# One chunk's state output product by Strassen's identity, with its block sums made beside the matmuls

## The chip, the cores and the metric

The kernel runs on one core of a Trainium2 chip. The metric is device time in microseconds (us). TensorE (PE) multiplies, VectorE (DVE) and ScalarE (ACT) do elementwise work, GpSimd (POOL) and SyncE (SP) issue most of the DMAs. The engines run beside one another and meet only at semaphores. TensorE writes into PSUM, which has eight banks of 128 partitions by 512 float32.

## The reference

A sequence of 2048 tokens of 512 features is normalized. Beside a residual connection it goes through a state space layer (A) and a gated feed-forward layer (B), and the three are added.

```python
def reference(A_x, ...):
    def _A_ref(x, ...):
        Lam_bar = jnp.exp(dt * Lam)
        B_bar = ((Lam_bar - 1.0) / Lam)[:, None] * Bmat
        Bu = jnp.einsum("bld,pd->blp", x + 0j, B_bar)
        for t in range(L):
            h = Lam_bar[None, :] * h + Bu[:, t, :]
            hs.append(h)
        hseq = jnp.stack(hs, 1)
        return 2.0 * jnp.einsum("blp,dp->bld", hseq, Cmat).real + x * Dskip[None, None, :]

    def _B_ref(x, w_gate, w_up, w_down):
        return (_silu(x @ w_gate) * (x @ w_up)) @ w_down

    xn = _layernorm(A_x, axis=-1)
    return A_x + _A_ref(xn, ...) + _B_ref(xn, ...)
```

The state is complex with 512 entries, so the last product of A is a real one: 2048 tokens by 1024 (real and imaginary parts) times 1024 by 512.

## The kernel before

The 2048 tokens are four chunks of 512, and each chunk is four tiles of 128 tokens, numbered `n` = 0 to 15. For each chunk the kernel makes the input projection of the state (`bproj`), the recurrence on VectorE (a rotation, eight scans, a rotation back into `w_tiles[c]`, called `wt` in the profile), the gate and up projections (`gateup`), the down projection into one PSUM bank per tile, and at last adds the state's output product into the same bank (`out_ssm`): eight matmuls of 512 columns per tile, one for each 128 of the 1024 state rows, `wt` against `CF`. The last 96 of the 1376 features of the feed-forward layer are treated apart: they are moved by small DMAs into `gu_rows` and enter through 32-row matmuls (`out_rows`).

The order is written out by hand. VectorE's recurrence steps stand in a backlog; `pump` issues some of them between matmuls, and `need("ssm2")` issues all that are left of chunk 2. What an engine or a queue is given it does in that order.

The first half (chunks 0 and 1) comes up in `out_chunk(1)`, before chunk 3's gate and up projections. The outputs of tiles 0 to 7 are copied out of PSUM by ScalarE into a buffer `res` of the pool `opool`, which has six of them, and added into the output in HBM by an accumulating DMA on GpSimd's queue (`out_leave`); the output in HBM already holds the residual, and `skip_store` adds the skip term there. Chunks 2 and 3 come up at the end, in `out_pair(2)`: the eight tiles 8 to 15 take all eight PSUM banks, first ten down-projection matmuls for each (80 in all), then `out_rows`, then `out_ssm` for chunk 2 and for chunk 3. Chunk 2's tiles leave by `out_leave`; chunk 3's by a VectorE addition with `xn_end` (which by then holds skip and residual) and plain stores from ScalarE's and SyncE's queues. The last tile, 15, is treated apart, so that little is left behind the last matmul: VectorE adds its bank to `xn_end` into `part_end` before the state product, and the state product goes into three fresh banks of 256, 128 and 128 columns, the blocks of `out_blocks`.

`CT` holds the transposed raw `C`, from which `CF` is made on VectorE during chunk 0. `BT` holds the transposed `B` for `bproj`; after the last `bproj` its real part is overwritten with the last rows of the down weights (`wd_rows`). `wg_g[2]` and `wu_g[2]` hold the gate and up weights of four of the eleven feature tiles; chunk 3's projection is their last reader. `jidx` is a float32 tile of 128x512, read only when the tables of sines are made, early. `pm` is a pool of three VectorE buffers of 4 KB per partition.

Of the kernel before, what the change touches and what calls it, by code (L numbers as in the profile page):

```python
# [10 lines left out]
F32 = mybir.dt.float32  # L11
BF16 = mybir.dt.bfloat16
ALU = mybir.AluOpType
ACT = mybir.ActivationFunctionType
# [9 lines left out]
def kernel(  # L24
# [17 lines left out]
    nc = tc.nc  # L42
    _, L, D = A_x.shape
# [4 lines left out]
    HW = CW // 2  # L48
    NT = L // 128
    NCH = L // CW  # L50
    TPC = CW // 128
    KD = D // 128
    HK = KD // 2
    NQ = Pst // 128
# [11 lines left out]
    ssm = ctx.enter_context(tc.tile_pool(name="ssm", bufs=1))  # L66
    gut = ctx.enter_context(tc.tile_pool(name="gut", bufs=2))
    up_p = ctx.enter_context(tc.tile_pool(name="up_p", bufs=4))
    opool = ctx.enter_context(tc.tile_pool(name="opool", bufs=6))
# [4 lines left out]
    def bank(shape=(128, CW), dtype=F32):  # L74
        return psum.tile(list(shape), dtype, name="ps")

    def flat(ap3):
        return ap3.rearrange("p q j -> p (q j)")

    x_v = A_x[0].rearrange("(n p) d -> p n d", p=128)  # L80
    out_v = out[0].rearrange("(n p) d -> p n d", p=128)
# [8 lines left out]
    wg_g, wu_g = [], []  # L90
# [7 lines left out]
    BT = const.tile([128, 2, KD, Pst], BF16, name="BT")  # L98
    CT = const.tile([128, 2, NQ, D], BF16, name="CT")
# [3 lines left out]
    CF = const.tile([128, 2, NQ, D], BF16, name="CF")  # L103
# [12 lines left out]
    HD = D // 2  # L116
# [51 lines left out]
    jidx = const.tile([128, CW], F32, name="jidx")  # L168
# [7 lines left out]
    part_end = const.tile([128, D], F32, name="part_end")  # L176
# [22 lines left out]
    xn_end = const.tile([128, TPC, D], BF16, name="xn_end")  # L199
# [72 lines left out]
    V = nc.vector  # L272
# [99 lines left out]
    u_tiles, w_tiles = {}, {}  # L372
# [85 lines left out]
    def gu_tile(c):  # L458
        if c not in gu_tiles:
            gu_tiles[c] = gut.tile([128, FT - 1, CW], BF16, name="guT")  # L460
        return gu_tiles[c]

    def u_tile(c, fi):
        if (c, fi // 2) not in u_pair:
            u_pair[c, fi // 2] = up_p.tile([128, 2, CW], BF16, name="u2")
        return u_pair[c, fi // 2]

    def product(c, fi):
        g, u = gu_tile(c)[:, fi - 1:fi + 1, :], u_tile(c, fi)[:]
        products.append(lambda: V.tensor_tensor(out=g, in0=g, in1=u, op=ALU.mult))  # L470
# [23 lines left out]
    def up_halves():  # L494

        pss = []
        for c in range(0, NCH, 2):
            ps = bank()
            pss.append(ps)
            for k in range(KD):  # L500
                for i in range(2):
                    nc.tensor.matmul(ps[i * LB:(i + 1) * LB], lhsT=wu_last[:, k, :],  # L502
                                     rhs=xnT[:, k, (c + i) * CW:(c + i + 1) * CW], start=(k == 0), stop=(k == KD - 1))
        for c in range(NCH):
            i = c % 2
            nc.scalar.copy(out=ul(c)[0:LB, :], in_=pss[c // 2][i * LB:(i + 1) * LB])
        product_last(0)
        product_last(1)
# [36 lines left out]
    o_tiles = {}  # L545

    def out_blocks(n):

        return ((0, D // 2), (D // 2, D - 128), (D - 128, D)) if n == NT - 1 else ((0, D),)

    def out_rows(c, step):

        for i in range(TPC):
            n, rows = c * TPC + i, slice(i * RT, (i + 1) * RT)
            nc.tensor.matmul(o_tiles[n][0][:], lhsT=gu_rows[c][rows, step, :], rhs=wd_rows[rows, step, :],  # L555
                             start=False, stop=(step == 2 and (c == 0 or n == NT - 1)))

    def out_pair(c):

        multiply(0)  # L560
        for n in range(c * TPC, (c + 2) * TPC):
            o = bank()
            o_tiles[n] = [o]
            k, i = divmod(n, TPC)
            for fi in range(FT - 1):
                nc.tensor.matmul(o[:], lhsT=gu_tiles[k][:, fi, i * 128:(i + 1) * 128], rhs=wd_sb[:, fi, :],  # L566
                                 start=(fi == 0), stop=False)
            pump(FT * 0.2163)
        for step in range(3):
            for k in (c, c + 1):  # L570
                out_rows(k, step)
        need(f"ssm{c}")
        need("skip")
        for n in range(c * TPC, (c + 1) * TPC):
            out_ssm(n)
            pump(2 * NQ * 0.2163)
        need(f"ssm{c + 1}")
        n = NT - 1
        o = o_tiles[n][0]
        V.tensor_tensor(out=part_end[:], in0=o[:], in1=xn_end[:, TPC - 1, :], op=ALU.add)  # L580
        o_tiles[n] = [bank((128, hi - lo)) for lo, hi in out_blocks(n)]
        for n in range((c + 1) * TPC, (c + 2) * TPC):
            out_ssm(n)

    def out_ffn(n):
        c, i = divmod(n, TPC)
        o_tiles[n] = []
        for lo, hi in out_blocks(n):
            o = bank((128, hi - lo))
            o_tiles[n].append(o)  # L590
            for fi in range(FT - 1):
                nc.tensor.matmul(o[:], lhsT=gu_tiles[c][:, fi, i * 128:(i + 1) * 128], rhs=wd_sb[:, fi, lo:hi],  # L592
                                 start=(fi == 0), stop=False)

    def out_ssm(n):
        c, i = divmod(n, TPC)
        if c > 0:
            res = opool.tile([128, D], BF16, name="res")
        for o, (lo, hi) in zip(o_tiles[n], out_blocks(n)):
            fresh = n == NT - 1  # L600
            o = o[:, 0:hi - lo]
            for part in range(2):
                for q in range(NQ):
                    nc.tensor.matmul(o, lhsT=w_tiles[c][:, part, q, i * 128:(i + 1) * 128],  # L604
                                     rhs=CF[:, part, q, lo:hi], start=(fresh and part == 0 and q == 0),
                                     stop=(c > 0 and part == 1 and q == NQ - 1))
            if c == NCH - 1:
                rest = part_end[:, lo:hi] if fresh else xn_end[:, i, lo:hi]
                V.tensor_tensor(out=res[:, lo:hi], in0=o, in1=rest, op=ALU.add)  # L609
                for a, b in ((0, D // 2), (D // 2, D)) if i == 0 else ((lo, hi),):  # L610
                    late = b == D and n in (NT - TPC, NT - 1)
                    (nc.sync if late else nc.scalar).dma_start(out=out_v[:, n, a:b], in_=res[:, a:b])
            elif c > 0:
                out_leave(n, o, res)

    def out_leave(n, o, res):
        nc.scalar.copy(out=res[:], in_=o[:])  # L617
        nc.gpsimd.dma_start(out=out_v[:, n, :], in_=res[:], accum_op=ALU.add)  # L618
# [14 lines left out]
    def step():  # L633
        for item in backlog[0:AHEAD + 1]:
            if item[2] is not None:
                item[2]()
                item[2] = None
        cost, op, _, _ = backlog.pop(0)
        op()
        owed[0] -= cost  # L640

    def pump(us):

        owed[0] += us
        while backlog and owed[0] >= backlog[0][0] * 0.5:
            step()
        if not backlog:
            owed[0] = 0.0

    def multiply(keep):  # L650

        while len(products) > keep:
            products.pop(0)()
            owed[0] -= 0.65

    def need(tag):

        while any(item[3] == tag for item in backlog):
            step()
# [135 lines left out]
    for fis in (range(4, EARLY - 1), range(EARLY - 1, EARLY)):  # L795
        ps, n = bank(), len(fis)
# [21 lines left out]
    def out_chunk(c):  # L818

        multiply(0)  # L820
        for n in range(c * TPC, (c + 1) * TPC):
            out_ffn(n)
            pump(FT * 0.2163)
        if c == 0:
            need("ln3")
            up_halves()
            multiply(0)
        if c == 1:
            for step in range(3):
                for k in range(2):  # L830
                    out_rows(k, step)
            for n in range(TPC):
                out_leave(n, o_tiles[n][0], opool.tile([128, D], BF16, name="res"))
        need(f"ssm{c}")
        need("cf")
        for n in range(c * TPC, (c + 1) * TPC):
            out_ssm(n)
            pump(2 * NQ * 0.2163)
# [46 lines left out]
    nc.sync.dma_start(out=out[0, 0:(NT - TPC) * 128, :], in_=A_x[0, 0:(NT - TPC) * 128, :])  # L885
    queue_ssm(2)
    out_chunk(0)
    gateup_chunk(2)
    bproj_chunk(3)
    load_rows()  # L890
    for c in range(NCH):
        queue("skip", [(1.2, lambda c=c: skip_op(c)),
                       (0.0, lambda c=c: skip_store(c)) if c < NCH - 1 else (1.2, skip_add)])
    queue_ssm(3)
    out_chunk(1)
    gateup_chunk(3)
    out_pair(2)


# [28 lines left out]
```

## Time and profile before

| | us |
|---|---|
| median of the three timed runs | 178.75 |
| the three runs | 178.48 to 178.84 |
| span of the profiled execution, first to last instruction | 176.8 |

The timed figure covers some 2 us around the span. The profile is of one execution. It is read from the page (busy times, the chain of work that ended last, the costliest groups) and from answers of the trace: the timeline, in which successive instructions of one kind are merged into a row with their count, groups of instructions by shape, and DMAs with their time from the start of the issuing instruction to landing. A matmul's shown length holds the way through the array, so rows of matmuls are read by the distance of their starts.

### The profile page before, as it was taken

Reading aid. Unit: us, or ns where it says so; the run is one execution under the profiler, and the core shown is the slowest. Engines: PE = TensorE matmul, PEld = TensorE weight load, DVE = VectorE, ACT = ScalarE, POOL = GpSimd, SP = SyncE. Lnnn points to the kernel's source line nnn. Section 1 sums busy time; section 2 is a strip of 40 time slices with the busy share of each in tenths; the row PEclk is TensorE's granted clock in tenths of the full one; section 3 lists DMA queues with packets and bytes.
Section 4 is the critical chain, followed back from the end, with each engine's and each line's share of the span. In section 5 each row is a group of like instructions: output and inputs, shape, how many; then the busy total and the mean of one; then the engine's idle time right before and its main releaser. Section 6 shows DMA issues by size and latency. Waiting matters only on the chain.

```text
span 176.8 us, 2598 instructions
## 1 busy us (share of the span) xinstructions
PE 172.1 (97%) x939; PEld 83.4 (47%) x954; DVE 153.8 (87%) x235; ACT 96.4 (55%) x178; POOL 51.8 (29%) x86
## 2 busy tenths in 40 slices
PE   8999999999999999999999999999999999999993
PEld 3877544444444444444444444444444444444443
DVE  4779998999999997999999999999999999981033
ACT  5397899867698679714666661053866610001300
POOL 6050120001400220019998040058476510001410
PEclk9999999999999999999999999999999999999999
DMA  5998497995431013900000020029799300000652
GB/s 164 305 186 197 91 247 97 336 272 117 88 73 21 0 30 89 356 4 17 17 19 19 0 85 7 0 23 126 88 126 188 64 6 0 0 4 0 64 99 75
DMA packets 31292, 16.36 MB, mean 92 GB/s; under 512 B 20208, under 2 KB 31088, under 8 KB 31248
## 3 DMA queue, kind: packets, MB, share of 16 engines
q1 hardware_dynamic: 24704, 11.51, 27.5%
q0 software_dynamic: 5184, 4.07, 16.0%
q10 hardware_dynamic: 1392, 0.62, 1.2%
q8 instruction: 7, 0.11, 0.3%
q14 instruction: 5, 0.04, 0.1%
HBM read 8.33 MB, written 5.24 MB: 77 GB/s over the span
## 4 chain that ended last, share of the span: by engine, by line
PE 94%; DMA 2%; issue 1%; SPq 0%; DVE 0%
PE ps L455 35%; PE ps L604 16%; PE ps L380 16%; PE ps L566 10%; PE ps L592 10%; DMA wu<-in_B_w_up_dram 2%; PE ps L693 2%; PE ps L513 2%; PE ps L774 2%; PE ps L555 2%; PE ps L502 1%; PE ps L245 0%; SPq L113 0%; SPq L123 0%; DVE res L609 0%
## 5 line engine op out<-in xcount | busy, mean ns | idle before, releaser
L455 PE MATMUL ps<-xnT,wu 128*128 128x512 bf16 (+1 forms) x144 | 36.3, 373 | 0.2
L455 PE MATMUL ps<-xnT,wg 128*128 128x512 bf16 (+1 forms) x145 | 36.3, 373 | 0.2
L422 DVE TENSOR_TENSOR_SCAN g<-r_t,car,u 128x512 bf16<-128x512 f32 x24 | 28.8, 1263 | 0.0
L380 PE MATMUL ps<-xnT,BT 128*128 128x512 bf16 x126 | 28.2, 379 | 0.1
L604 PE MATMUL ps<-CF,wt 128*128 128x512 bf16 (+2 forms) x140 | 27.6, 355 | 0.4 <-issue 0.3
L474 ACT ACTIVATE guT<-ps 128x512 bf16<-128x512 f32 (+1 forms) x40 | 23.6, 590 | 5.9 <-PE ps L455 5.8
L475 ACT CAST u<-ps 128x512 bf16<-128x512 f32 (+1 forms) x40 | 23.0, 576 | 6.5 <-PE ps L455 6.4
L617 ACT CAST res<-ps 128x512 bf16<-128x512 f32 x12 | 6.7, 590 | 36.1 <-PE ps L604 26.8
L455 PEld LDWEIGHTS <-wu 128*128 128x128 bf16 x148 | 14.5, 98 | 16.6
L188 POOL DMA_DIRECT2D gu_rows<-ul x36 | 17.7, 499 | 15.8 <-DVE ul L490 15.8
L455 PEld LDWEIGHTS <-wg 128*128 128x128 bf16 x148 | 14.4, 98 | 16.5
L382 ACT CAST u<-ps 128x512 bf16<-128x512 f32 x32 | 18.2, 586 | 6.0 <-PE ps L380 5.9
L618 POOL DMA_DIRECT2D out_dram<-res x12 | 10.5, 1221 | 36.2 <-ACT res L617 36.1
L604 PEld LDWEIGHTS <-wt 128*128 128x128 bf16 x144 | 13.3, 98 | 15.0 <-issue 1.3
L380 PEld LDWEIGHTS <-BT 128*128 128x128 bf16 x128 | 12.5, 98 | 14.9 <-issue 0.3
L214 POOL TENSOR_TENSOR rstd<-ve,neg_half 128x2 f32<-128x2 f32 (+1 forms) x4 | 5.7, 1418 | 44.9 <-DVE ve L213 44.9
L592 PE MATMUL ps<-wd_sb,guT 128*128 128x512 bf16 x79 | 17.5, 379 | 0.1
L566 PE MATMUL ps<-wd_sb,guT 128*128 128x512 bf16 x79 | 17.4, 379 | 0.1
L470 DVE TENSOR_TENSOR guT<-guT,u 128x1024 bf16<-128x1024 bf16 x20 | 13.4, 678 | 0.0
L566 PEld LDWEIGHTS <-guT 128*128 128x128 bf16 x80 | 7.8, 98 | 9.5
L592 PEld LDWEIGHTS <-guT 128*128 128x128 bf16 x80 | 7.8, 98 | 9.5
L205 DVE BATCH_NORM_STATS2 stats<-xall 128x6 f32<-128x512 bf16 x14 | 9.5, 678 | 2.7 <-DMA xall<-in_A_x_dram 2.7
(125 smaller groups left out, 201.4 us busy)
## 6 DMA issues: line engine op xcount, KB each, us to landing
out_dram<-in_A_x_dram SPq DMA_DIRECT2D x1, 1536.0 KB, 6.9
out_dram<-res POOLq DMA_DIRECT2D x12, 128.0 KB, 3.5
out_dram<-xall POOLq DMA_DIRECT2D x3, 512.0 KB, 8.4
wd_sb<-in_B_w_down_dram SPq DMA_DIRECT2D x2, 640.0 KB, 8.2
xall<-in_A_x_dram SPq DMA_DIRECT2D x1, 1024.0 KB, 7.1
gu_rows<-ul POOLq DMA_DIRECT2D x36, 8.0 KB, 1.6
wg<-in_B_w_gate_dram SPq DMA_DIRECT2D x1, 512.0 KB, 4.7
wu<-in_B_w_up_dram SPq DMA_DIRECT2D x1, 512.0 KB, 5.5
```

The lines of the kernel that those rows point to most:

```text
L188: nc.gpsimd.dma_start(out=gu_rows[c][i * RT:(i + 1) * RT, p, :], in_=product[p * RT:(p + 1) * RT, i * 128:(i + 1) * 128])
L380: nc.tensor.matmul(ps[:], lhsT=BT[:, part, k, q * 128:(q + 1) * 128], rhs=xnT[:, k, c * CW:(c + 1) * CW], start=(k == 0), stop=(k == KD - 1))
L382: nc.scalar.copy(out=u_tiles[c][:, part, q, :], in_=ps[:])
L422: V.tensor_tensor_scan(out=g()[:, part, q, :], data0=r_t[:, q:q + 1].to_broadcast([128, CW]), data1=u_tiles[c][:, part, q, :], initial=ini ...
L455: nc.tensor.matmul(ps[:fs, lo:hi], lhsT=wslice(groups, fi, k), rhs=xnT[:, k, c * CW + lo:c * CW + hi], start=(k == 0), stop=(k == KD - 1))
L470: products.append(lambda: V.tensor_tensor(out=g, in0=g, in1=u, op=ALU.mult))
L474: nc.scalar.activation(out=gu_tile(c)[:, fi, 0:hi], in_=psg[:, 0:hi], func=ACT.Silu)
L475: nc.scalar.copy(out=u_tile(c, fi)[:, fi % 2, 0:hi], in_=psu[:, 0:hi])
L566: nc.tensor.matmul(o[:], lhsT=gu_tiles[k][:, fi, i * 128:(i + 1) * 128], rhs=wd_sb[:, fi, :], start=(fi == 0), stop=False)
L592: nc.tensor.matmul(o[:], lhsT=gu_tiles[c][:, fi, i * 128:(i + 1) * 128], rhs=wd_sb[:, fi, lo:hi], start=(fi == 0), stop=False)
L604: nc.tensor.matmul(o, lhsT=w_tiles[c][:, part, q, i * 128:(i + 1) * 128], rhs=CF[:, part, q, lo:hi], start=(fresh and part == 0 and q == 0 ...
L618: nc.gpsimd.dma_start(out=out_v[:, n, :], in_=res[:], accum_op=ALU.add)
```

## The change

Strassen's identity multiplies two matrices of 2x2 blocks with seven block products instead of eight, with sums of blocks ahead of and behind them. Here (the variant of Winograd) the left matrix is chunk 2's state, 512 tokens by 1024 rows: `a11` is the real part for the first 256 tokens, `a12` the imaginary part for them, `a21` and `a22` the same for the other 256. The right matrix is `CF`: `b11` and `b12` are the left and right 256 columns for the real part, `b21` and `b22` for the imaginary part. One block product is two token tiles by four state tiles, eight matmuls of 256 columns; chunk 2's 32 matmuls of 512 columns become 56 of 256. Chunk 3 keeps its ordinary product.

- The sums of blocks of `CF` (`t1` to `t4`, and the negated `b22`) are made in `out_chunk(1)`, behind chunk 3's `bproj`: five ScalarE copies with a sign into `CT` and into the imaginary part of `BT`, then five accumulating DMAs of 256 KB from SBUF to SBUF on GpSimd's queue. The last two wait for `t3` and `t4` to land. On GpSimd's queue they stand behind `load_rows` and ahead of the eight output DMAs of tiles 0 to 7.
- The sums of blocks of the state (`s1` to `s4`) are made in the same way in `out_pair`, into `wg_g[2]` and `wu_g[2]`: four ScalarE copies behind the last eviction of chunk 3's projections, then four accumulating DMAs; `s2` takes in the landed `s1`, and `s4` the landed `s2`. On GpSimd's queue they stand behind the moves of `gu_rows` for chunk 3.
- Four of the seven products go into PSUM banks of their own, taken one after the other; the first two of these are banks that are freed early by evicting tile 15 and now also tile 14 (into `jidx`). Three products accumulate straight into the tiles' banks. ScalarE copies two of the four out; VectorE adds the others to what is there (`u2`, `low`, `high`, in `pm` buffers).
- The four tiles of chunk 2 leave together behind the products: VectorE adds the bank and the sums into `res`, and GpSimd's accumulating DMA stores it. The four ScalarE copies that did this are gone. A `res` buffer comes round after six tiles: tile 14 is written where tile 8 was, tile 15 where tile 9 was.
- The state product of tile 14 now also starts in a fresh bank, as that of tile 15 did.

```diff
+    def weight_sums():
+        (b11, b12), (b21, b22) = BQ
+        t1, t2, t3, t4 = TQ
+        for out, in_, sign in ((t1, b11, -1.0), (t3, b12, -1.0), (t4, b22, -1.0), (t2, b11, 1.0),
+                               (neg_b22, b22, -1.0)):
+            nc.scalar.activation(out=out, in_=in_, func=ACT.Copy, scale=sign)
+        for out, in_ in ((t1, b12), (t3, b22), (t4, b21), (t2, t3), (t4, t1)):
+            add_dma(out, in_)
...
+    def state_sums(c):
+        (a11, a12), (a21, a22) = state_quarters(c)
+        s1, s2, s3, s4 = SQ
+        for out, in_, sign in ((s1, a21, 1.0), (s2, a11, -1.0), (s3, a21, -1.0), (s4, a12, -1.0)):
+            nc.scalar.activation(out=out, in_=in_, func=ACT.Copy, scale=sign)
+        for out, in_ in ((s1, a22), (s3, a11), (s2, s1), (s4, s2)):
+            add_dma(out, in_)
+
+    def out_ssm_seven(c):
...
+        def product(a, b, place, start, stop):
+            for i in range(2):
+                for q in range(NQ):
+                    nc.tensor.matmul(place(i), lhsT=a[:, q, i * 128:(i + 1) * 128], rhs=b[:, q, :],
+                                     start=(start and q == 0), stop=(stop and q == NQ - 1))
...
+        product(a12, b21, at(0, 0), False, False)
+        product(a22, t4, at(1, 0), False, True)
+        x, place = taken()
+        product(a11, b11, place, True, True)
+        nc.scalar.copy(out=low[:, :, 0, :], in_=x[:])
+        x, place = taken()
+        product(s1, t1, place, True, True)
+        nc.scalar.copy(out=five, in_=x[:])
+        x, place = taken()
+        product(s2, t2, place, True, True)
+        V.tensor_tensor(out=u2, in0=x[:], in1=low[:, :, 0, :], op=ALU.add)
+        V.tensor_tensor(out=low[:, :, 1, :], in0=u2, in1=five, op=ALU.add)
+        x, place = taken()
+        product(s3, t3, place, True, True)
+        product(s4, neg_b22, at(0, 1), False, True)
+        V.tensor_tensor(out=high[:, :, 0, :], in0=x[:], in1=u2, op=ALU.add)
+        V.tensor_tensor(out=high[:, :, 1, :], in0=high[:, :, 0, :], in1=five, op=ALU.add)
+
+        for half, extra in ((0, low), (1, high)):
+            for i in range(2):
+                n = first + 2 * half + i
+                res = opool.tile([128, D], BF16, name="res")
+                V.tensor_tensor(out=res[:], in0=o_tiles[n][0][:], in1=flat(extra[:, i]), op=ALU.add)
+                nc.gpsimd.dma_start(out=out_v[:, n, :], in_=res[:], accum_op=ALU.add)
 
     def out_pair(c):
 
         multiply(0)
+        for n in [*parts, *range(c * TPC, NT - len(parts))]:
+            o_tiles[n] = [bank()]
+        state_sums(c)
...
         need(f"ssm{c}")
         need("skip")
-        for n in range(c * TPC, (c + 1) * TPC):
-            out_ssm(n)
-            pump(2 * NQ * 0.2163)
         need(f"ssm{c + 1}")
-        n = NT - 1
-        o = o_tiles[n][0]
-        V.tensor_tensor(out=part_end[:], in0=o[:], in1=xn_end[:, TPC - 1, :], op=ALU.add)
-        o_tiles[n] = [bank((128, hi - lo)) for lo, hi in out_blocks(n)]
+        for n, part in parts.items():
+            V.tensor_tensor(out=part[:], in0=o_tiles[n][0][:], in1=xn_end[:, n - NT + TPC, :], op=ALU.add)
+        out_ssm_seven(c)
         for n in range((c + 1) * TPC, (c + 2) * TPC):
+            if n in parts:
+                o_tiles[n] = [bank((128, hi - lo)) for lo, hi in out_blocks(n)]
             out_ssm(n)
...
     def out_chunk(c):
 
         multiply(0)
+        if c == 1:
+            weight_sums()
```

`parts` is `{15: part_end, 14: jidx}`, `at(half, h)` names a half of a tile's bank, `taken()` a fresh bank, and `add_dma` is a DMA on GpSimd's queue with `accum_op=ALU.add`.

More of the change, by code (lines that the diff above doesn't have):

```diff
@@ L555, in out_rows @@
             nc.tensor.matmul(o_tiles[n][0][:], lhsT=gu_rows[c][rows, step, :], rhs=wd_rows[rows, step, :],
-                             start=False, stop=(step == 2 and (c == 0 or n == NT - 1)))
+                             start=False, stop=(step == 2 and (c == 0 or n in parts)))
+    BQ = [[CF[:, j, :, h * HD:(h + 1) * HD] for h in range(2)] for j in range(2)]
+    TQ = [CT[:, i // 2, :, (i % 2) * HD:(i % 2 + 1) * HD] for i in range(4)]
+    neg_b22 = BT[:, 1, :, 0:HD]
+    SQ = [(wg_g, wu_g)[i // 2][2][:, :, (i % 2) * HD:(i % 2 + 1) * HD] for i in range(4)]
@@ new lines, with add_dma @@
+    parts = {NT - 1: part_end, NT - 2: jidx}
+    def add_dma(out, in_):
+        nc.gpsimd.dma_start(out=out, in_=in_, accum_op=ALU.add)
+    def weight_sums():
[6 more added lines that the diff above has]
+            add_dma(out, in_)
@@ new lines, in state_quarters @@
+    def state_quarters(c):
+        w = w_tiles[c]
+        return [[w[:, j, :, h * HW:(h + 1) * HW] for j in range(2)] for h in range(2)]
+    def state_sums(c):
[5 more added lines that the diff above has]
+            add_dma(out, in_)
@@ new lines, in out_ssm_seven, with at, taken @@
+    def out_ssm_seven(c):
+        (a11, a12), (a21, a22) = state_quarters(c)
+        (b11, b12), (b21, b22) = BQ
+        (s1, s2, s3, s4), (t1, t2, t3, t4) = SQ, TQ
+        first = c * TPC
+        def product(a, b, place, start, stop):
[3 more added lines that the diff above has]
+                                     start=(start and q == 0), stop=(stop and q == NQ - 1))
+        def at(half, h):
+            return lambda i: o_tiles[first + 2 * half + i][0][:, h * HD:(h + 1) * HD]
+        def taken():
+            x = bank((128, 2, HD))
+            return x, lambda i: x[:, i, :]
+        low = ssm.tile([128, 2, 2, HD], F32, name="pm", bufs=3)
+        high = ssm.tile([128, 2, 2, HD], F32, name="pm", bufs=3)
+        both = ssm.tile([128, 2, 2, HD], F32, name="pm", bufs=3)
+        u2, five = both[:, 0], both[:, 1]
+        product(a12, b21, at(0, 0), False, False)
[21 more added lines that the diff above has]
+                nc.gpsimd.dma_start(out=out_v[:, n, :], in_=res[:], accum_op=ALU.add)
@@ L558, in out_pair @@
     def out_pair(c):
         multiply(0)
+        for n in [*parts, *range(c * TPC, NT - len(parts))]:
+            o_tiles[n] = [bank()]
+        state_sums(c)
         for n in range(c * TPC, (c + 2) * TPC):
-            o = bank()
-            o_tiles[n] = [o]
+            o = o_tiles[n][0]
             k, i = divmod(n, TPC)
@@ L599, in out_ssm @@
         for o, (lo, hi) in zip(o_tiles[n], out_blocks(n)):
-            fresh = n == NT - 1
+            fresh = n in parts
             o = o[:, 0:hi - lo]
@@ L607, in out_ssm @@
             if c == NCH - 1:
-                rest = part_end[:, lo:hi] if fresh else xn_end[:, i, lo:hi]
+                rest = parts[n][:, lo:hi] if fresh else xn_end[:, i, lo:hi]
                 V.tensor_tensor(out=res[:, lo:hi], in0=o, in1=rest, op=ALU.add)
```

## The prediction

> **What bounds the kernel now.** First the page: the span, the busy line and the chain of work that ended last.
>
> ```profile
> span 176.8 us, 2598 instructions
> PE 172.1 (97%) x939; PEld 83.4 (47%) x954; DVE 153.8 (87%) x235; ACT 96.4 (55%) x178; POOL 51.8 (29%) x86
> ...
> PE 94%; DMA 2%; issue 1%; SPq 0%; DVE 0%
> ```
>
> TensorE fills the span and is 94% of the chain, so a microsecond of matmul that goes is a microsecond won, if the work that the change adds stays behind it and the last output leaves as soon after the last matmul as now. Hence the timeline from 157 us on, where the changed stage lies. Columns: start, length, engine, line, operation, and in brackets the idle time before it.
>
> ```profile
> 157.45 1.23 DVE L404 TENSOR_TENSOR wt<-pm 128x2048 bf16<-128x2048 bf16 x1
> ...
> 160.06 13.86 PEld L604 LDWEIGHTS <-wt 128*128 128x128 bf16 x80 [0.42 <-issue]
> 160.18 0.69 DVE L580 TENSOR_TENSOR part_end<-ps,xn_end 128x512 f32<-128x512 f32 x1 [1.50 <-PE ps L555]
> 160.29 13.80 PE L604 MATMUL ps<-CF,wt 128*128 128x512 bf16 x78 [0.16 <-issue]
> 162.00 0.58 ACT L617 CAST res<-ps 128x512 bf16<-128x512 f32 x1 [19.92 <-PE ps L604]
> 162.88 0.90 POOL L618 DMA_DIRECT2D out_dram<-res  x1 [20.71 <-ACT res L617]
> ...
> 168.90 0.69 DVE L609 TENSOR_TENSOR res<-ps,xn_end 128x512 bf16<-128x512 f32 x1 [8.03 <-PE ps L604]
> ...
> 172.41 0.69 DVE L609 TENSOR_TENSOR res<-ps,xn_end 128x512 bf16<-128x512 f32 x1 [1.09 <-PE ps L604]
> 173.29 0.68 DVE L609 TENSOR_TENSOR res<-ps,part_end 128x256 bf16<-128x256 f32 x2 [0.18 <-PE ps L604]
> 174.12 0.29 DVE L609 TENSOR_TENSOR res<-ps,part_end 128x128 bf16<-128x128 f32 x1 [0.16 <-PE ps L604]
> ```
>
> The reader is to see four things. TensorE runs the two chunks' 80 state matmuls without a break from 160.07 (two records are missing, 78 of 80; the first weights come at 160.06). Its results are read about 0.20 us after the last matmul was fed: eight matmuls of 0.216 end at 161.80, ScalarE starts at 162.00. ScalarE, GpSimd and VectorE are idle for 19.92, 20.71 and 8.03 us ahead of their first work of this stage. And VectorE's last addition ends at 174.41, 2.4 us before the span does; that rest (the last store) is the same in both kernels.
>
> **The matmuls.** The change takes out 32 matmuls of 512 columns and puts in 7 x 8 = 56 of 256.
>
> ```profile
> 31.80 6.91 PE ps L380 x32
> ...
> L604 PEld LDWEIGHTS <-wt 128*128 128x128 bf16 x144 | 13.3, 98 | 15.0 <-issue 1.3
> ```
>
> 32 wide ones take 6.91 us (the chain in order of time), 0.216 each. A narrow one is half of that, 0.108, or by the last tile's first block (172.41 to 173.29 for eight) 0.110. So 56 cost 6.05 to 6.16 us, and TensorE saves 0.75 to 0.87. I take **-0.85**, nearer to the even half, since the 0.88 holds a seam between tiles. A weight load, 98 ns, goes with each and is shorter than its matmul.
>
> The Trainium skill, page "TensorE: Matmul & The Clock Gate", section "Back-to-back issue gap", speaks against this: in a stream of load and matmul pairs it has about 131 ns for 512 columns and about 81 for 128. By that 32 wide ones would be 4.2 us, 56 narrow ones at an estimated 98 ns 5.5 us, and the change would lose 1.3 us. The trace differs from it on both sides: 216 ns for 512 columns, and 52 ns for 128 (173.29 to 174.12 for 16).
>
> **Banks inside the seven products.** The third product takes the bank of the last tile, which VectorE's eviction frees at 160.87; the fourth that of the last tile but one, whose added eviction (another 0.69) ends at 161.56. They are needed at 161.80 and 162.66. The first could slip 0.9 us before TensorE waits; VectorE's own chain ends at 158.68, 1.5 us before the eviction can start. The fifth product (nominal start 163.53) takes the bank that ScalarE copies out after the third: fed until 162.66, copy from 162.86, 0.58 long, free at 163.44. The sixth likewise after the fourth. That is 0.09 us of room for a semaphore's way, which no row shows; below nothing is excluded, as waiting can only add. Nothing to 0.2; I take **+0.05**.
>
> **The state sums** (four ScalarE casts of 128x1024, four accumulating DMAs of 256 KB) start where ScalarE ends its last eviction of chunk 3 (162.00 - 19.92 = 142.08) and GpSimd its last row move (162.88 - 20.71 = 142.17).
>
> ```profile
> L319 ACT ACTIVATE c<-pm 128x1024 bf16<-128x1024 f32 x2 | 2.2, 1076 | 0.0
> L315 DVE SCALAR_TENSOR_TENSOR pm<-pm 128x1024 f32<-128x1024 f32 x4 | 4.9, 1226 | 0.1
> ```
>
> A cast of that shape costs about 1.08, so they end at 146.4, in idle time. The trace has no accumulating DMA into SBUF. The nearest are those into HBM:
>
> ```profile
> out_dram<-res POOLq DMA_DIRECT2D x4, 128.0 KB, 3.1
> ...
> L618 POOL DMA_DIRECT2D out_dram<-res x1: 1240/1240/1240, 117.6 to 117.6; - x1
> ...
> DMA to landing us min/median/max: 3.8/3.8/3.8
> ...
> L542 POOL DMA_DIRECT2D out_dram<-xall x3: 1300/1460/1627, 127.2 to 129.5; - x3
> ...
> DMA to landing us min/median/max: 6.3/8.4/9.9
> ```
>
> 128 KB land 3.1 us after the issue begins (the four in the tail, one at a time), 3.8 where one began 0.6 us ahead, and 512 KB 6.3 with nothing ahead. The three 512 KB stores landed from 133.5 (127.2 + 6.3) to 139.4 (129.5 + 9.9), 3.0 us apart. 256 KB lie between; I take 4.7. The second sum adds the first, the fourth the second: three in a row from 143.45 (first cast, and 0.30 from its end to GpSimd's start, as 162.58 to 162.88). They land at 157.6, or at 162.4 with 6.3 each; the seventh product wants the last at 165.26. TensorE's down-projection hides it all. **0**; the cover is gone at 7.3 us a DMA, and from there every 0.1 costs 0.3.
>
> **The weight sums** go through ScalarE and GpSimd while chunk 1's outputs come up.
>
> ```profile
> 116.12 2.65 ACT L617 CAST res<-ps 128x512 bf16<-128x512 f32 x5 [9.23 <-PE ps L555]
> ...
> 117.01 5.38 POOL L618 DMA_DIRECT2D out_dram<-res  x6 [11.91 <-ACT res L617]
> ...
> 121.68 0.58 ACT L617 CAST res<-ps 128x512 bf16<-128x512 f32 x1 [1.19 <-PE ps L604]
> ...
> 123.16 1.03 PE L513 MATMUL ps<-xnT,w_last 128*128 128x512 bf16 x4
> ```
>
> Five casts fit into ScalarE's 9.23 idle us from 106.89. Five DMAs stand on GpSimd's queue ahead of the eight output DMAs; two of them wait for a landing. At 4.7 us, and half of those 3.0 between landings, the last is issued at about 117, when the first output arrives: nothing lost. At 6.3 (3.0 apart) it is issued near 121.9; the seventh output copy (121.68 now), whose buffer waits for the first output's landing, comes 6 us late and ScalarE's gate-up evictions queue behind it. TensorE, taking a bank every 0.865 us from 123.16 on, comes to that tile's bank after six others, at 128.35, when the copy would just be done. So **0**, at the upper bound up to 0.5.
>
> **The way out.** This is where I expect a price. Before, chunk 2's four tiles left one by one, 1.73 us (eight matmuls) apart, by ScalarE. Now VectorE makes four sums and four outputs once the products are there, 0.69 each (a float32 pass over 1024 is 1226 ns, and 512 from PSUM 0.69). From the fifth product's result at 164.60: the sums end at 167.36, the four outputs at 168.05, 168.74, 169.43 and 170.12; tiles 12 and 13 follow to 171.50. Tile 14 is ready at 171.55 and the first block of tile 15 at 172.43, so VectorE's 8 idle us cover the eight passes. But `res` has six buffers. Tile 14 writes the buffer of tile 8 and tile 15 that of tile 9, and waits until that tile's DMA has landed. GpSimd starts tile 8's at 168.35 and it lands at 171.45, in time. Tile 9's arrives 0.69 later behind it, like the second DMA row above (117.6, the second of a series that began at 117.01): 3.8 us, 172.8. Tile 15 then starts at 172.8 instead of 172.43, its three blocks (0.42, 0.29, 0.29, overlapping a little) run without TensorE, and the end moves from 173.55 to 173.8. Without queueing (3.1) it costs nothing, with the longest of that series (5.2, its row under rival b) 1.7. I take the second row of the series, since this DMA is the second: **+0.25**.
>
> **Sum.** -0.85 + 0.05 + 0 + 0 + 0.25 = -0.55. The profiled span is 176.8, the timed runs' median 178.75; the 1.95 us around it stay. 178.75 - 0.55 = **178.2 us**.
>
> **The rivals.**
> (a) The gain is eaten: tile 9's DMA takes 3.9 to 4.7 us from its arrival. For it: the stores of tiles 12 and 13 now share the DMA engines with four accumulations. Against: alone this DMA takes 3.1. 178.4 to 179.1.
> (b) Slower, by that same wait: the series of output DMAs that starts at 117.0 goes up to
>
> ```profile
> DMA to landing us min/median/max: 3.0/4.1/5.2
> ```
>
> and at 5.2 tile 15 starts at 174.25 and ends at 175.25, 0.84 after now: 179.6. Slower from 174.4 on, that is a landing after 173.4, 4.4 us; measurably from 4.7. Against it: the 5.2 had four DMAs ahead of it, tile 9's has one.
> (c) The chain of state sums is late. At the 9.9 of the third 512 KB store it would land at 173.2, 8 us after its product: 186. Against: that one had 1 MB ahead.
> (d) The narrow matmuls don't run at half: if a load were not fetched ahead, 98 + 52 ns each is 8.4 us for 56, 1.5 more than the wide ones now, and the time 180.5 with the 0.3 of the waits; the break-even is 123 ns. Against: eight in 0.88. By the Trainium skill's "Back-to-back issue gap" above, which would be of this kind, the time would be about 180.
> (e) The weight sums hold up the gate-up evictions by their upper bound: 178.7.
>
> **How the numbers follow.** Forecast 53%, own range 177.85 (no wait anywhere) to 178.4; (a) 22%, (b) 12%, (c) 6%, (d) 3%, (e) 4%. A change under 0.2%, 0.36 us, can't be told from none. Faster: the forecast, 53%. Same: (a) and (e), 26%. Slower: (b), (c), (d), 21%. The range reaches from 177.85 up to 179.2, which takes in (a), (e) and the lower half of (b).
>
> **What would show it.** The seven products' first start to tile 12's first matmul: 6.1 us, against 6.9. A gap before the fifth or sixth product shows the bank term, one before the seventh the state sums. VectorE's last three passes back to back instead of waiting for TensorE, with a DMA as their releaser, show the `res` wait. Output copies and gate-up matmuls at 121 to 130 standing where they do now show the weight sums hidden. The prediction is wrong if TensorE stalls in the products, or if tile 9's DMA lands more than half a microsecond from 172.8.

## The result and the profile after

The changed kernel takes 180.94 us (median; 180.79 to 181.12) against 178.62 us (178.31 to 178.84) for the kernel before on the same chip: ratio 1.0146, 95% interval 1.0128 to 1.0164. It is slower by 2.3 us, where a gain of 0.55 us was forecast. First the page of the changed kernel: span, busy time and chain.

```profile
span 179.2 us, 2683 instructions
PE 171.5 (96%) x964; PEld 85.7 (48%) x978; DVE 159.0 (89%) x244; ACT 103.7 (58%) x185; POOL 63.3 (35%) x95
...
PE 75%; issue 10%; DMA 9%; POOL 1%; SPq 0%; DVE 0%; DVEq 0%; POOLq 0%
```

TensorE is busy 0.6 us less than before, yet the span is 2.4 us longer. The chain that ends last now holds 9% DMA and 10% issue, but it does not show the loss: it ends on VectorE at 173.80, 5.4 us short of the span's end. The timeline of the changed stage shows that the loss does not lie among the products. Columns as in the prediction.

```profile
160.09 1.05 PE L598 MATMUL ps<-CF,wt 128*128 128x256 bf16 x8
...
160.97 1.04 PE L598 MATMUL ps<-CT,wt 128*128 128x256 bf16 x8
161.84 1.04 PE L598 MATMUL ps<-CF,wt 128*128 128x256 bf16 x8
...
162.72 1.91 PE L598 MATMUL ps<-CT,wg 128*128 128x256 bf16 x16
...
164.47 1.04 PE L598 MATMUL ps<-CT,wu 128*128 128x256 bf16 x8
...
165.34 1.04 PE L598 MATMUL ps<-BT,wu 128*128 128x256 bf16 x8
...
166.10 7.04 PEld L683 LDWEIGHTS <-wt 128*128 128x128 bf16 x48
...
168.43 3.48 POOL L635 DMA_DIRECT2D out_dram<-res  x4 [13.32 <-DVE res L634]
...
172.98 0.82 DVE L688 TENSOR_TENSOR res<-ps,part_end 128x256 bf16<-128x256 f32 x3 [0.61 <-PE ps L683]
```

The seven products start every 0.875 us with no gap (the x16 row holds two), and tile 12's first weights follow at 166.10. VectorE's last addition ends at 173.80, 0.61 us earlier than the 174.41 of before. Up to there the change wins. From there to the end of the span it was 2.4 us before and is 5.4 us now.

What fills this stretch is seen in the instructions that close the program (they stand under the line that opens each kernel's context, L923 and L1004). Before, from 160 us to the end of SyncE's closing waits; columns: line, engine, operation, count, duration in ns (min/median/max), first and last start.

```profile
L923 SPq EVENT_SEMAPHORE  x9: 28/28/28, 174.8 to 175.9; - x9
L923 POOLq DRAIN  x1: 6748/6748/6748, 168.0 to 168.0; - x1
...
L923 SPq DRAIN  x1: 13/13/13, 176.0 to 176.0; - x1
```

The changed kernel, the same view:

```profile
L1004 SPq EVENT_SEMAPHORE  x9: 28/28/28, 175.1 to 176.1; - x9
L1004 POOLq DRAIN  x1: 8207/8207/8207, 170.2 to 170.2; - x1
...
L1004 SPq DRAIN  x1: 7/7/7, 176.2 to 176.2; - x1
```

GpSimd closes with an instruction called DRAIN that stands behind its last DMA issue; its record begins when that issue begins, so it is read by its end. Before, it ran from 168.03 to 174.78 and was over 1.2 us before SyncE had seen every DMA land (175.99), so it cost nothing. After, it runs from 170.20 to 178.41, 2.2 us past SyncE's 176.21. The rest of the program end, 0.79 us, follows it: 178.41 + 0.79 = 179.20, the span. GpSimd's closing semaphores, before and then after, come only when both its DRAIN and SyncE's waits are over:

```profile
L923 POOLq EVENT_SEMAPHORE  x4: 17/17/17, 176.1 to 176.7; - x4
```

```profile
L1004 POOLq EVENT_SEMAPHORE  x4: 17/17/17, 178.5 to 179.1; - x4
```

The waits of SyncE's queue say the same: after 173 us, before and then after, in all, times, longest:

```profile
SPq L923 <- PEq L923: 0.7, 2, 0.5
```

```profile
SPq L1004 <- PEq L1004: 2.9, 2, 2.3
```

Of SyncE's two waits for the other engines at the closing barrier, the second takes about 0.5 us in both kernels; the first grew from about 0.2 (0.7 - 0.5) to 2.3 us. The row names PEq, but the closing DRAIN of TensorE's weight loads ended at 173.4; at 176.3 only GpSimd's was still running. A DRAIN belongs to none of the rows of busy work, so neither the timeline nor the page's groups show it.

The last stores are slower too. DMA issues from 170 to 177 us, median us from issue to landing, before:

```profile
out_dram<-res ACTq DMA_DIRECT2D x2, 64.0 KB, 1.9
out_dram<-res ACTq DMA_DIRECT2D x1, 32.0 KB, 1.5
```

and after (beside these rows, the two 128 KB stores of ScalarE went from 1.7 to 3.3):

```profile
out_dram<-res POOLq DMA_DIRECT2D x3, 128.0 KB, 4.4
...
out_dram<-res ACTq DMA_DIRECT2D x2, 64.0 KB, 2.5
...
out_dram<-res ACTq DMA_DIRECT2D x1, 32.0 KB, 2.2
```

The stores of tiles 14 and 15 share the DMA engines with the accumulating ones, whose last packet ends at 174.74. The last landing comes 2.3 us after VectorE's last addition (176.07), against 1.5 before (175.91). So SyncE's waits end 0.2 us later than before although VectorE ends 0.6 us earlier; this lies under the DRAIN.

### The profile page after: what moved, and what is told of

It is laid out like the page before. It is cut to its first block, busy times and chain, and to the rows that moved or that the text cites. A ratio compares the mean times of both kernels' runs of the same rounds, so it can differ in the third digit from the quotient of the medians.

```text
span 179.2 us, 2683 instructions
## 1 busy us (share of the span) xinstructions
PE 171.5 (96%) x964; PEld 85.7 (48%) x978; DVE 159.0 (89%) x244; ACT 103.7 (58%) x185; POOL 63.3 (35%) x95
## 4 chain that ended last, share of the span: by engine, by line
PE 75%; issue 10%; DMA 9%; POOL 1%; SPq 0%; DVE 0%; DVEq 0%; POOLq 0%
PE ps L455 35%; PE ps L380 15%; PE ps L671 10%; PE ps L683 8%; DMA wu<-in_B_w_up_dram 2%; DMA wg<-wg 2%; PE ps L772 2%; DMA out_dram<-res 2%; PE ps L513 2%; DMA wg<-wt 2%; PE ps L853 2%; PE ps L502 1%; PE ps L555 1%; POOL wu L565 1%; DVE res L688 0%
## 5 line engine op out<-in xcount | busy, mean ns | idle before, releaser
L683 PE MATMUL ps<-CF,wt 128*128 128x512 bf16 (+2 forms) x109 | 20.8, 348 | 0.3 <-issue 0.2
L683 PEld LDWEIGHTS <-wt 128*128 128x128 bf16 x112 | 10.2, 98 | 10.9 <-issue 0.8
L616 ACT COPY pm<-ps 128x512 f32<-128x512 f32 x1 | 0.6, 585 | 17.0 <-PE ps L598 17.0
L390 DVE TENSOR_TENSOR pm<-g,c 128x2048 bf16<-128x2048 bf16 x8 | 9.7, 1219 | 0.1
```

What stands on the lines that cost most here:

```text
L390: V.tensor_tensor(out=t[:], in0=flat(src()[:, i]), in1=flat(tab[:]), op=ALU.mult)
```

## The experiments

Times are medians. Ratios are to the kernel before, measured beside each set (178.37 us for the first four, 178.24 for the next four, 178.36 for the last two).

**The DRAIN alone, without the change.** The kernel before, one plain store moved to GpSimd's queue:

```diff
-                    (nc.sync if late else nc.scalar).dma_start(out=out_v[:, n, a:b], in_=res[:, a:b])
+                    eng = nc.gpsimd if n == NT - 3 else nc.sync if late else nc.scalar
+                    eng.dma_start(out=out_v[:, n, a:b], in_=res[:, a:b])
```

> The kernel before, with one edit: tile 13's plain store (128 KB, ready at about 171.3 us) is issued by GpSimd instead of ScalarE. Theory (drain): the program cannot end before GpSimd's closing DRAIN does, and that ends some 6 us after GpSimd's last DMA issue (before: issue ended 168.90, drain ended 174.78, span 176.8; after: 171.91, 178.41, 179.2). Here the last issue ends near 172.5, so the drain ends at 178.3 to 179.0 and the span at 179.0 to 179.8: 180.7 to 181.6 us, though no computation is added. Rival (bytes): the end is late because of what the last stores and accumulations move; the same bytes leave at the same moment here, so 178.6, unchanged. Rival (number): the drain is longer because the changed kernel has issued nine more DMAs on GpSimd's queue; here 178.6 too.

180.75 us, ratio 1.0127 (1.0104 to 1.0149): one late issue on GpSimd costs what the whole change costs. Both rivals had 178.6 and fall. VectorE ends at 174.07 and SyncE's waits at 175.7; the DRAIN ends at 177.80, 5.96 behind the last issue. That issue came earlier than expected, so the DRAIN's end missed the expected 178.3 to 179.0, though the time lies within its range.

```profile
L924 SPq DRAIN  x2: 7/7/7, 175.7 to 175.8; - x2
L924 POOLq DRAIN  x1: 6552/6552/6552, 171.3 to 171.3; - x1
```

**The change without late GpSimd DMAs.** Chunk 2's outputs as plain stores from SyncE. It leaves out the residual and skip part of tiles 8 to 11.

```diff
-                nc.gpsimd.dma_start(out=out_v[:, n, :], in_=res[:], accum_op=ALU.add)
+                nc.sync.dma_start(out=out_v[:, n, :], in_=res[:])
```

> The changed kernel, with chunk 2's four outputs stored by plain DMAs from SyncE instead of accumulating ones from GpSimd; it leaves out the addition of residual and skip to tiles 8 to 11. Theory (drain): GpSimd's last DMA is then the last state sum (issue ends 155.1), its drain is over by about 162 and sets nothing; the span ends 2.4 us after VectorE's last addition, which is at 173.5 to 173.7: span 175.9 to 176.2, time 177.7 to 178.1. Rival (bytes): the same 512 KB are stored at the same time, so most of the 2.3 us stay: 180 to 181. Rival (number): the nine sums are still on GpSimd's queue: 180.9.

178.10 us, ratio 0.9982 (0.9967 to 0.9996). The DRAIN is over at 161.84:

```profile
L1004 POOLq DRAIN  x1: 8311/8311/8311, 153.5 to 153.5; - x1
```

From the first state matmul to VectorE's end it takes 13.56 us against 14.34 before: a gain of 0.78 us, of which 0.3 shows in the time. The rest goes behind the last landing: that comes 1.52 us after VectorE's end (1.50 before), but SyncE's waits end 0.54 us after the landing (0.08 before).

**The same with the full result.** The residual of chunk 2 is added in SBUF by an accumulating load, and VectorE adds it into the PSUM banks in time in which it was idle. For that the seventh product moves up to third place, and `x` is no longer copied into the output for chunk 2:

```diff
+        if c == NCH - 2:
+            nc.gpsimd.dma_start(out=xall[:, c * TPC:(c + 1) * TPC, :], in_=x_v[:, c * TPC:(c + 1) * TPC, :],
+                                accum_op=ALU.add)
+            return
...
+        for n in (first + 2, first + 3, first, first + 1):
+            V.tensor_tensor(out=o_tiles[n][0][:], in0=o_tiles[n][0][:], in1=xall[:, n, :], op=ALU.add)
...
-                nc.gpsimd.dma_start(out=out_v[:, n, :], in_=res[:], accum_op=ALU.add)
+                nc.sync.dma_start(out=out_v[:, n, :], in_=res[:])
```

> The changed kernel with its whole result, but chunk 2's residual and skip are gathered in SBUF (one accumulating load of x into the tile that holds the skip term, in place of the third accumulating store), VectorE adds them to the four banks while it waits for the products (the seventh product is moved up to third), and the four outputs leave by plain stores from SyncE. Theory (drain): no late DMA on GpSimd, so the end follows VectorE again: its last addition at 173.5 to 173.8, time 177.7 to 178.2, below the kernel before. Rivals (bytes, number): 180 to 181.

178.42 us, ratio 0.9998 (0.9981 to 1.0015): below the rivals' 180 to 181, but above the range of 177.7 to 178.2, which had no place for SyncE's waits. VectorE again ends 13.56 us after the stage's start, but the 0.78 us are gone at the end. The last landing is at 174.91, and SyncE's closing waits end only at 175.7:

```profile
L1010 SPq EVENT_SEMAPHORE  x9: 27/28/28, 173.7 to 175.6; - x9
L1010 POOLq DRAIN  x1: 8417/8417/8417, 153.4 to 153.4; - x1
...
L1010 SPq DRAIN  x1: 7/7/7, 175.7 to 175.7; - x1
```

**The wait for `res` in tile 15.** The changed kernel with buffers of their own for the outputs of tiles 14 and 15:

```diff
-        if c > 0:
+        if n >= NT - 2:
+            res = up_p.tile([128, 2, CW], BF16, name="u2")[:, 0, :]
+        elif c > 0:
```

> The changed kernel with buffers of their own for the outputs of tiles 14 and 15, so that tile 15 does not wait for tile 9's accumulating DMA. Theory (drain): VectorE's last addition comes 0.2 to 0.4 earlier (173.4 to 173.6 instead of 173.8), and the time does not move, since GpSimd's drain sets the end: 180.7 to 181.1. Rival (the wait for the buffer reaches the end, as I priced it): 180.5 to 180.7.

180.86 us, ratio 1.0138 (1.0114 to 1.0163), the changed kernel's. VectorE ends 13.56 us after the stage's start instead of 13.71, so the wait was real and worth 0.15 us, but the DRAIN (to 178.23) sets the end.

**Order of the closing waits.** The kernel with the residual in SBUF, its four stores of chunk 2 split over two queues:

```diff
-                nc.sync.dma_start(out=out_v[:, n, :], in_=res[:])
+                nc.sync.dma_start(out=out_v[:, n, 0:HD], in_=res[:, 0:HD])
+                nc.scalar.dma_start(out=out_v[:, n, HD:D], in_=res[:, HD:D])
```

> The kernel with chunk 2's residual in SBUF (178.42 us), its four stores each cut into two column halves, one issued by SyncE and one by ScalarE. Full result. VectorE's last addition should end 13.5 to 13.6 us after the stage's first matmul, as there. Theory A (what is lost of the 0.78 us is the order in which SyncE's closing waits come: one that is met late holds the others, about 0.5 to 0.8 us behind the last landing): eight more hardware DMAs shift that order, SyncE's closing waits end within 0.2 us of the last landing, and the time is 177.6 to 178.0 us. Theory B (the closing waits start late for a reason that has nothing to do with their order): 178.2 to 178.6 us. Theory C (ScalarE's four issues hold back its copies or evictions in the last stage): VectorE ends later and the time is above 178.6.

177.58 us, ratio 0.9964 (0.9949 to 0.9979): the lower edge of theory A's range, and faster than the kernel before and the changed one. VectorE ends at 173.20, 13.57 after the stage's start, the last store lands at 174.81, and SyncE is through at once:

```profile
L1011 SPq EVENT_SEMAPHORE  x9: 28/28/28, 173.6 to 174.8; - x9
...
L1011 SPq DRAIN  x1: 7/7/7, 174.9 to 174.9; - x1
```

**The four stores by ScalarE**, unsplit (`nc.scalar` for `nc.sync` in the same line):

> The same kernel with the four stores of chunk 2 issued by ScalarE in place of SyncE, unsplit; SyncE's own number of closing waits stays as it is. Full result. Theory A (order of the closing waits): the number of hardware DMAs is unchanged, so the waits keep their gap of 0.5 to 0.8 us and the time stays at 178.2 to 178.6. Theory B (SyncE's own queue of issues delays its closing waits): 177.6 to 178.0.

177.83 us, ratio 0.9969 (0.9956 to 0.9983). Theory A had 178.2 to 178.6, so it missed here, and B's range held. The waits one by one show that both had a part. SyncE waits for its semaphores in a fixed order, about 0.065 us each. With four unsplit stores the last landing belongs to the fifth of the nine waits, and what is behind it still has to be gone through: 0.3 us from the landing (175.21) to the end (175.54). With SyncE issuing the stores a pause of 0.47 us comes on top, ahead of the sixth wait, though all that this wait names had landed 2.7 us before. The pause stands at the same wait in the split version, where the last two waits have to stay for later landings anyway, and it is missing where SyncE has four issues fewer. In the version without the residual, where SyncE also issues the four stores, a pause of 0.46 us stands ahead of the fifth wait. What it is was not settled.

**Fewer GpSimd issues.** The changed kernel, two accumulating output DMAs of 256 KB in place of four of 128 KB:

```diff
+            pair = up_p.tile([128, 2, CW], BF16, name="u2")
...
-                res = opool.tile([128, D], BF16, name="res")
-                V.tensor_tensor(out=res[:], in0=o_tiles[n][0][:], in1=flat(extra[:, i]), op=ALU.add)
-                nc.gpsimd.dma_start(out=out_v[:, n, :], in_=res[:], accum_op=ALU.add)
+                V.tensor_tensor(out=pair[:, i, :], in0=o_tiles[n][0][:], in1=flat(extra[:, i]), op=ALU.add)
+            nc.gpsimd.dma_start(out=out_v[:, n - 1:n + 1, :], in_=pair[:], accum_op=ALU.add)
```

> The changed kernel with two accumulating output DMAs of 256 KB for chunk 2 (tiles 8 and 9, tiles 10 and 11) in place of four of 128 KB. Full result. VectorE's last addition should end as in the changed kernel or up to 0.3 us earlier. If GpSimd's closing DRAIN sets the end and ends 5.9 to 7 us after its last issue: the last issue is earlier by one issue of about 1 us, the DRAIN ends at 177.2 to 178.0 and the time is 179.8 to 180.6 us. If the DRAIN follows the last packet (3.5 to 3.9 us behind it) and the packets of the 256 KB come as late as those of the 128 KB: 180.7 to 181.1 us. If the bytes of the accumulation set the end in another way than by the DRAIN: 181 or more.

181.56 us, ratio 1.0177 (1.0151 to 1.0202), slower still and above both times expected with a DRAIN. The last issue ends 0.46 us earlier than in the changed kernel (171.46), but its last packet ends 0.8 us later (175.53), where the later of these times had assumed that it comes no later, and the DRAIN ends at 179.12, 3.6 us behind that packet. The span's end, 179.91, follows the DRAIN by 0.79 as in the changed kernel, so the DRAIN still sets it; but issue time alone is not the rule.

**Fewer bytes.** The kernel before, 16 of 128 partitions of tile 13's output by GpSimd, the rest by ScalarE:

```diff
+                    if n == NT - 3:
+                        nc.scalar.dma_start(out=out_v[0:112, n, a:b], in_=res[0:112, a:b])
+                        nc.gpsimd.dma_start(out=out_v[112:128, n, a:b], in_=res[112:128, a:b])
+                        continue
```

> The kernel before, with 16 of 128 partitions of tile 13's output stored by GpSimd and the other 112 by ScalarE: 16 KB of plain store in place of the 128 KB of the earlier run, issued as late. Full result. Theory (GpSimd's closing DRAIN ends some 6 us behind its last issue, whatever the bytes): the DRAIN ends at 177 to 178 and the time is 180.3 to 181.0 us. Rival (the DRAIN waits for bytes and for landing only): the DRAIN ends by 176 and the time is 178.3 to 178.9.

180.34 us, ratio 1.0117 (1.0093 to 1.0142), against 1.0127 with eight times the bytes. The rival falls: the DRAIN ends at 177.72, 5.95 us behind the issue, as with 128 KB.

**Earlier and later.** The kernel before with another store on GpSimd, the second half of tile 12 (`n == NT - 4 and b == D`) or tile 14 (`n == NT - 2`):

> The kernel before, with the second half of tile 12's output (64 KB, plain store) issued by GpSimd in place of SyncE: some 1.7 us earlier than the store of tile 13 that GpSimd issued in an earlier run. Full result. Theory (GpSimd's closing DRAIN ends 5.9 to 6.0 us behind the end of its last issue, and nothing of it shows while it ends before SyncE's closing waits, which end at 176.0): the last issue ends at 170.1 to 170.3, the DRAIN at 176.0 to 176.3, so that it has just come out from under its cover, and the time is that of before to 0.4 us more: 178.2 to 178.7 us. Rival (any GpSimd store in the last stage costs about 2.4 us, wherever it stands): 180.4 to 181.0.

> The kernel before, with tile 14's output (128 KB, plain store) issued by GpSimd in place of ScalarE: some 1.8 us later than tile 13's. Full result. Theory: the last issue ends at 173.6 to 173.9, the DRAIN at 179.5 to 179.9, the program ends 0.8 us behind it, and the time is 4.0 us above before less the 0.2 that tile 12 leaves: 182.0 to 182.6 us. Rival (any GpSimd store in the last stage costs about 2.4 us): 180.4 to 181.0.

178.78 us, ratio 1.0025 (1.0008 to 1.0042), and 182.00 us, ratio 1.0196 (1.0173 to 1.0220). Both lie at the edge of the theory's range, the first 0.1 us above it, and far from the rival's constant cost: tile 12's store should have cost 2.4 us by it and cost 0.4, tile 14's cost 3.6. The closing instructions of the kernel with tile 12:

```profile
L924 SPq DRAIN  x2: 7/7/7, 175.9 to 176.0; - x2
L924 POOLq DRAIN  x1: 6548/6548/6548, 169.7 to 169.7; - x1
```

and with tile 14:

```profile
L924 POOLq DRAIN  x1: 6552/6552/6552, 172.9 to 172.9; - x1
```

With tile 12 the DRAIN (to 176.26) has just come out from under SyncE's waits (175.92), and the time is 0.4 us longer; with tile 13 it is 2.4, with tile 14 3.6. All of it in one table, us from the span's start:

| kernel | last GpSimd issue ends | its last packet ends | DRAIN ends | SyncE's waits end |
|---|---|---|---|---|
| before | 168.91 | 170.85 | 174.78 | 175.99 |
| tile 12 by GpSimd | 170.30 | 171.29 | 176.26 | 175.92 |
| tile 13, 16 KB | 171.77 | 172.76 | 177.72 | 175.62 |
| tile 13, 128 KB | 171.85 | 172.93 | 177.80 | 175.7 |
| tile 14 | 173.52 | 174.66 | 179.47 | 175.70 |
| changed kernel | 171.92 | 174.74 | 178.41 | 176.21 |
| two merged sums | 171.46 | 175.53 | 179.12 | 176.96 |
| residual in SBUF | 154.73 | 158.32 | 161.86 | 175.71 |

In every row the DRAIN ends at the later of two times: about 5.9 us after the last issue (the plain stores, and before), or about 3.6 us after the last packet (the accumulating DMAs whose packets come late). That form was fitted to these runs after the fact. The dependence on the issue's time was forecast for tiles 12 and 14 and came within 0.1 us of the forecast ranges; the 3.6 us after the last packet were not tested by a run of their own. What the DRAIN does in this time no run shows.

## Why the prediction was wrong

**The step that failed** is in the first part: "VectorE's last addition ends at 174.41, 2.4 us before the span does; that rest (the last store) is the same in both kernels." The rest was not the last store alone. It was the later of the last store's landing and GpSimd's DRAIN, and only 1.2 us lay between them. The change moved GpSimd's last issue by 3.0 us (168.91 to 171.92) and its DRAIN's end by 3.6, so 3.6 - 1.2 = 2.4 us came out: the loss, by itself. The rows were there: the prediction has the four outputs leave by GpSimd from 168.35 on, and an issue takes 0.87, so the last one ends near 171.8. With the 5.9 us that the trace of before shows from its last issue to the DRAIN's end, 0.85 to the span's end and 1.95 around it, that is 180.5 us. (The DRAIN in fact ended 6.5 us behind that issue, as its packets came late.) None of the rivals had this mechanism, and the signs of being wrong that the prediction names, a stall in the products or a late landing of tile 9's DMA, did not come up: both lie ahead of VectorE's last addition, and the loss behind it.

**Matmuls: -0.85 forecast.** The seven products take 6.12 us (160.09 to 166.21; the first matmul of tile 12 has no record, and a weight load stands 0.11 ahead of its matmul) against 6.92: -0.80. A 256-column matmul took 0.109 us, between the two values weighed. Rival (d) falls. The figures that the Trainium skill, "TensorE: Matmul & The Clock Gate", "Back-to-back issue gap", has for a stream of load and matmul pairs (131 ns for 512 columns, 81 for 128) do not hold for this kernel: it took 216 and 52.

**Banks: +0.05 forecast**, 0 measured: no gap at the third to the sixth product.

**State sums: 0 forecast**, right. In the changed kernel the accumulating DMAs into SBUF (the line's instructions; the first two groups are the weight sums, the third is the fourth state sum):

```profile
L565 POOL DMA_DIRECT2D CT<-CF x3: 1349/1716/2067, 108.2 to 110.1; - x3
L565 POOL DMA_DIRECT2D CT<-CT x2: 1255/1260/1265, 115.4 to 117.1; - x2
...
L565 POOL DMA_DIRECT2D wu<-wg x1: 1265/1265/1265, 153.8 to 153.8; - x1
...
DMA to landing us min/median/max: 4.2/4.5/6.5
```

Over all nine, 256 KB land in a median of 4.5 us (4.7 assumed). The last of the four is issued at 153.84 and lands at 158.9, 6 us before the seventh product. Rival (c) falls.

**Weight sums: 0 forecast**, right: the last is issued at 117.14 and the first output DMA follows at 117.89, 0.9 later than before; the gate-up matmuls start at 123.19, as before (123.16). Rival (e) falls.

**Tile 15's wait: +0.25 forecast**, 0.15 by the run with own buffers. Tile 9's DMA landed at 172.86 (172.8 forecast), 3.83 us after its issue began, as the changed kernel's chain in order of time has it:

```profile
169.03 3.83 DMA out_dram<-res
```

VectorE's additions for tile 15 follow at 172.98; the bracket of that row names TensorE, but the chain and the run with own buffers, where they start without this wait, show the DMA. VectorE ended at 173.80, as forecast. That is luck: without the wait it would have ended 0.1 later than the 173.55 forecast, and the wait cost 0.1 less. Rivals (a) and (b) priced the right wait too high, and at the measured landing it would not have mattered, since the DRAIN sets the end.

**The last store.** Even with the DRAIN out of the way the landing 0.8 us slower behind VectorE would have taken the gain: SyncE's waits end 0.2 us later than before. So the failed step, that the rest behind VectorE is the same, is wrong twice. What the seven products are worth shows only where chunk 2's outputs leave as plain stores by the hardware queues and SyncE's waits don't stand behind the landing: 0.36% (0.21 to 0.51) against before, 0.66 us of the 0.78 that the stage gains. That version differs from the kernel before in more than the products; the residual's new way was not tried alone.

## What to carry to other kernels

Before calling the end of a kernel unchanged, look at the closing instructions of every engine, not at the busy rows: which one ends last, and by how much the next is hidden. In these runs a plain store issued by GpSimd near the end brought a DRAIN that ended 5.9 to 6.0 us behind the issue, with 16 KB as with 128 KB, so the last outputs went better by the queues of SyncE and ScalarE. A shorter TensorE stage is worth only what the way out lets through: of the four versions without late GpSimd DMAs, all with its 0.78 us at VectorE's end, two lost more than half of it between the last landing and the end of SyncE's waits.

## What had not been expected of the hardware

- GpSimd's DRAIN ended 5.88 to 5.96 us after the last issue in five kernels (the kernel before and those with one plain store of 16 to 128 KB), and 3.5 to 3.7 us after the last packet in the seven kernels with the block sums.
- SyncE's nine closing waits took about 0.065 us each in a fixed order, so it mattered which of them the last landing belonged to (0.3 us behind the fifth, 0.1 behind the ninth), and a pause of 0.46 to 0.48 us appeared with four more issues on SyncE; its cause is open.
- Beside accumulating DMAs into HBM the last plain stores of ScalarE took 2.2 us instead of 1.5 (32 KB), 2.5 instead of 1.9 (64 KB) and 3.3 instead of 1.7 (128 KB); in the version without those DMAs they took 1.5, 1.7 and 1.7.
